# Attention and a rational MLP on one core: the last 64 keys' exponentials are added to the sum tiles by GpSimd instead of being summed by TensorE

## The chip, the core and the metric

The kernel runs on one core of a Trainium2 chip. The metric is device time in microseconds for one execution, median of three runs. TensorE (PE) multiplies matrices, VectorE (DVE) and ScalarE (ACT) work on tiles, GpSimd (POOL) and SyncE (SP) mostly issue DMAs here. Every engine runs its instructions in the order in which they were written, and waits for the others by semaphores. TensorE's weight loads (PEld) are shown beside its products.

## What is computed

Four batches of twelve heads, 448 tokens, head dimension 64. The twelve heads' outputs are put side by side and go through an MLP with a rational activation.

```python
scores = cap * np.tanh(scale * np.matmul(q, k.transpose(0, 1, 3, 2)) / cap)
attn = np.exp(scores - np.max(scores, axis=-1, keepdims=True))
attn = attn / (np.sum(attn, axis=-1, keepdims=True) + 1e-09)
x = np.matmul(attn, v)                 # (4, 12, 448, 64) -> (1792, 768)
h = x @ w_in                           # 768 -> 2048
P = a[0] + a[1] * h + a[2] * h**2 + a[3] * h**3
Q = 1.0 + abs(b[0]) * abs(h) + abs(b[1]) * h**2
out = (P / (Q + 1e-06)) @ w_out        # 2048 -> 768
```

## The kernel before

**Units.** `attention` goes over 24 head pairs p (two heads each). The 448 keys of a head pair are four tiles: n = 0, 1, 2 of 128 keys each, and the last 64 keys, n = 3, for which an even and the next odd head pair share one tile of 128 partitions (64 each). Two head pairs so form a pair k = p // 2, twelve in all. For each tile: `scores` (six products, twelve for n = 3) writes a bank of `ps`, `softmax` has ACT take tanh and then exp into `etiles` (L440, L457). Since the cap bounds the scores, no maximum is subtracted.

**The sums.** For each head pair DVE adds the exponentials of n = 0, 1, 2 into a sum tile `es` (two adds, L463; six such tiles, in `arena_f` and `extra`). The denominators are products of these tiles with a matrix of ones: `norm4` (L594) takes two pairs at once in three rounds of four products into `mi` (plain fp32: each shows as two records in the trace, eight a round). Rounds one and two read the sum tiles, round three reads the shared tiles of the last 64 keys. It stands at p = 5, 9, 13, 17 and 21, behind the scores of n = 3. `norm` (L556) does one pair in two rounds of four, the second over the last 64 keys; it stands at p = 23 for pair 10, and behind the attention for pair 11.

**Behind the sums.** DVE copies `mi` to SBUF (L598), POOL sends it by four small DMAs into a layout of 56 columns, DVE takes the reciprocal (L606), POOL stores it to DRAM (`dn`) and reads it back as broadcasts (`arena_r<-dn`), and DVE multiplies the attention output by them (`xout`, L627). Between these POOL also loads the V rows of the last 64 keys (`ring<-in_v`, `load32`), which wait for the products that read the ring before (L528).

**Other work of a head pair.** `prep_k` and `prep_q` transpose the keys and queries of a later head pair into a bank of `ps` (L343 to L366), from which DVE makes four tiles (L350, L381, L351, L384); the bank is wanted again by that visit's or the next one's third group of scores. `pv` (L511) and `pv_tails` (L528) multiply by V into `pv` and `mi`, which DVE copies out (L535). `split_x` makes an upper part (ACT, L638) and a lower part (DVE, L639) of each 128-column slice of x, and weights are made from 64-bit words early on (L789 to L822).

**The MLP.** `stage1` multiplies a slice of x (upper, lower, upper) with a weight's parts into `ps`, 896 tokens wide, as 512 and 384 columns. For units 0 to 3 it goes slice by slice with the widths in turn (L858); from unit 4 on all 18 products of one width stand in a row (L843). `rational` (L889 to L902) makes the activation, `stage2` (L928) multiplies by w_out. Units 0 and 1 need the first half of the tokens, units 2 and 3 the second, whose last two slices wait for pair 11's denominators.

**What sets the order.** `visits` lists, for each head pair, the functions in order; all TensorE work carries a key `turn`, so TensorE keeps this order. `Plan.flush` then simulates the five engines with the costs given to `op` (`SC_NS`, `PV_NS`, `D_NS`, ...), and writes each engine's instructions in the order in which they start there: the costs decide how ACT's, DVE's, POOL's and SP's rows interleave.

Of the kernel before, what the change touches and what calls it, by code (L numbers as in the profile page):

```python
# [16 lines left out]
ALU = mybir.AluOpType  # L17
# [30 lines left out]
FILL = (4, 4)  # L48
# [24 lines left out]
class Plan:  # L73
# [174 lines left out]
class Body:  # L248
# [11 lines left out]
    def __init__(self, tc, io, cst, bounded):  # L260
# [71 lines left out]
    def prep_k(self, p):  # L332
# [16 lines left out]
        self.op(PE, 440 + SHAPE_NS, tk, self.raw_keys(p, "rk"), [bk, "turn"], early=E_TR)  # L349
# [4 lines left out]
    def prep_q(self, p):  # L354
# [19 lines left out]
        self.op(PE, 390, tq, self.raw_keys(p, "rq"), [bq, "turn"], early=E_TR)  # L374
# [40 lines left out]
    def scores(self, p, n):  # L415
# [15 lines left out]
        first = n == 0 or p % 2 and n == 2  # L431
        self.op(PE, SC_NS * len(sets) + TURN_NS * first, run, [k for name, _ in sets for k in K(name)], w, early=E_SC)

    def softmax(self, p, n):
# [6 lines left out]
        if self.bounded:  # L441
            self.exp(p, n, e, [ek], e, ek)

    def etile(self, p, n):
# [4 lines left out]
        return self.e[ie], ("e", ie)  # L449

# [46 lines left out]
    def pv(self, p):  # L497
# [16 lines left out]

        self.op(PE, PV_NS + SHAPE_NS, run, [("rv", ring_of(g), 0)] + [t[1] for t in tiles], [pk, "turn"])

    def pv_tails(self, p):
# [14 lines left out]
        self.op(PE, TAIL_NS, run, [("v32", ring_of(g), 0), ("v32", ring_of(g), 1), ek], ["pv", "mi", "turn"])  # L532
# [5 lines left out]
    def norm(self, k):  # L538
# [10 lines left out]

        def sums():  # L550
            for last in range(2):
                for j in range(2):
                    for x in range(2):
                        h = 32 * (2 * j + x)
                        st, mv = (self.half[x], tail[:, j]) if last else (self.ones, es[x][:, j])
                        m = nc.tensor.matmul(D[h:h + 32], st, mv, start=not last, stop=last == 1)  # L556
            return m

        self.op(PE, D_NS + SHAPE_NS, sums, [("es", (2 * k + x) % NES) for x in range(2)] + [tk, "ones"], [dk, "turn"])
# [20 lines left out]
    def norm4(self, k):  # L580
# [4 lines left out]
        tails = [self.etile(2 * (k + y), 3) for y in range(2)]  # L585
# [748 lines left out]
```

## Time and profile before

| | us |
|---|---|
| median of 3 runs (lowest to highest) | 660.5 (659.9 to 661.07) |
| the profiled execution | 659.91 |
| its span, first to last instruction | 657.9 |

| engine | busy us | share of the span |
|---|---|---|
| PE | 647.8 | 98% |
| PEld | 542.0 | 82% |
| DVE | 541.9 | 82% |
| ACT | 442.2 | 67% |
| POOL | 85.0 | 13% |

The granted TensorE clock is 0.999 of full speed. Busy times are unions of the instructions' spans; PE's ends are modelled, so the start of the next instruction is the surer end of one. Attention takes the span up to some 184 us, the passage (units 0 to 3 of the MLP) up to some 220, the rest is the MLP.

### The profile page before, as it was taken

How to read it: one execution, taken by the hardware profiler on the slowest of the kernel's cores; microseconds unless marked ns; L12 is line 12 of the kernel's file. 1: busy time of each engine (PE TensorE's matmuls, PEld its weight loads, DVE VectorE, ACT ScalarE, POOL GpSimd, SP SyncE). 2: the span in 40 equal slices, each digit the busy share in tenths (PEclk: the TensorE clock that was granted, in tenths of full speed). 3: DMA queues.
4: the chain of work that ended last, by engine and by line, in shares of the span. 5: the costliest groups of instructions: out<-in, count | busy, mean ns of one | idle time of the engine just before them, and what ended most of it. 6: DMA issues, size and time to landing. Idle time of an engine off the chain costs nothing.

```text
span 657.9 us, 9767 instructions
## 1 busy us (share of the span) xinstructions
PE 647.8 (98%) x3820; PEld 542.0 (82%) x3820; DVE 541.9 (82%) x662; ACT 442.2 (67%) x531; POOL 85.0 (13%) x141
## 2 busy tenths in 40 slices
PE   8999999999999999999999999999999999999996
PEld 5555555655478899999999999999999999999996
DVE  4789899899679987977987897899699789969653
ACT  5899999999857867875457466646646565663560
POOL 4013222321200000020012002101200210120030
PEclk9999999999999999999999999999999999999999
DMA  7757864943230332195158118614821671481086
GB/s 170 186 138 171 203 163 100 199 119 85 59 86 22 128 141 92 51 197 113 48 106 158 49 49 152 158 43 86 166 68 49 128 142 60 95 170 33 1 139 203
DMA packets 79095, 74.45 MB, mean 113 GB/s; under 512 B 48456, under 2 KB 67264, under 8 KB 79040
## 3 DMA queue, kind: packets, MB, share of 16 engines
q1 hardware_dynamic: 68240, 48.68, 25.7%
q0 software_dynamic: 9648, 24.80, 22.5%
q8 instruction: 32, 0.52, 0.3%
q10 hardware_dynamic: 1152, 0.25, 0.2%
q14 instruction: 23, 0.19, 0.1%
HBM read 47.98 MB, written 25.65 MB: 112 GB/s over the span
## 4 chain that ended last, share of the span: by engine, by line
PE 82%; DVE 6%; ACT 4%; DMA 3%; issue 3%; POOL 0%; SPq 0%; DVEq 0%; POOLq 0%; ACTq 0%
PE ps L843 31%; PE ps L928 17%; PE mi L928 9%; PE pv L928 9%; PE ps L429 6%; PE mi L511 3%; DMA arena_r<-dn 2%; ACT etiles L440 2%; PE mi L594 1%; PE pv L511 1%; ACT etiles L457 1%; PE pv L528 1%; PE ps L343 1%; DMA dn<-arena_f 1%; PE ps L366 1%
## 5 line engine op out<-in xcount | busy, mean ns | idle before, releaser
L843 PE MATMUL ps<-arena_r,ring 128*128 128x512 f32 (+1 forms) x924 | 207.6, 363 | 0.0
L843 PEld LDWEIGHTS ps<-arena_r,ring 128*128 128x128 f32 x924 | 167.7, 188 | 17.5
L295 POOL DMA_DIRECT2D out_dram<-arena_f x49 | 42.0, 863 | 423.6 <-ACT arena_f L955 423.6
L928 PE MATMUL ps<-arena_r,etiles 128*128 128x384 f32 x462 | 89.7, 335 | 0.6 <-ACT arena_f L955 0.5
L457 ACT ACTIVATE etiles<-etiles,acap 128x896 f32<-128x896 f32 x84 | 85.5, 1053 | 0.2
L440 ACT ACTIVATE etiles<-ps 128x896 f32<-128x896 f32 x84 | 74.7, 921 | 13.9 <-PE ps L429 13.7
L928 PEld LDWEIGHTS ps<-arena_r,etiles 128*128 128x128 f32 x462 | 80.8, 188 | 1.3 <-ACT arena_f L955 0.8
L928 PE MATMUL mi<-arena_r,etiles 128*128 128x384 f32 x231 | 77.2, 336 | 0.0
L928 PE MATMUL pv<-arena_r,etiles 128*128 128x384 f32 x231 | 77.0, 335 | 0.0
L429 PEld LDWEIGHTS ps<-arena_r 64*128 64x128 f32 x576 | 51.0, 184 | 25.2 <-ACT etiles L457 7.8
L889 ACT ACTIVATE arena_f<-ps,b 128x896 f32<-128x896 f32 x32 | 32.3, 1009 | 54.8 <-PE ps L843 54.7
L429 PE MATMUL ps<-arena_r 64*128 64x448 f32 x576 | 67.7, 376 | 1.2 <-DVE arena_r L384 0.9
L789 ACT ACTIVATE arena_f<-arena_f 128x768 f32<-128x768 f32 x32 | 29.4, 918 | 44.1 <-DMA arena_f<-in_moe_w_out_dram 31.0
L901 ACT CAST etiles<-arena_f 128x896 fp32r<-128x896 f32 x32 | 30.3, 946 | 42.0 <-DVE arena_f L900 42.0
L893 DVE SCALAR_TENSOR_TENSOR arena_f<-arena_f,bab 128x896 f32<-128x896 f32 x32 | 36.8, 1150 | 23.8 <-ACT arena_f L890 23.8
L898 DVE SCALAR_TENSOR_TENSOR arena_f<-arena_f,one 128x896 f32<-128x896 f32 x32 | 36.7, 1148 | 11.3 <-ACT arena_f L896 11.3
L928 PEld LDWEIGHTS pv<-arena_r,etiles 128*128 128x128 f32 x231 | 43.3, 188 | 0.6
L928 PEld LDWEIGHTS mi<-arena_r,etiles 128*128 128x128 f32 x231 | 43.3, 188 | 0.6
L928 PE MATMUL ps<-ring,etiles 128*128 128x384 f32 x210 | 42.0, 334 | 0.0
L902 DVE TENSOR_TENSOR etiles<-arena_f,etiles 128x896 fp32r<-128x896 f32 x32 | 34.9, 1089 | 7.0 <-ACT etiles L901 6.8
L891 ACT ACTIVATE arena_f<-ps,a 128x896 f32<-128x896 f32 x32 | 35.3, 1104 | 3.5 <-DVE arena_f L899 3.5
L897 DVE SCALAR_TENSOR_TENSOR arena_f<-arena_f,a,ps 128x896 f32<-128x896 f32 x32 | 36.6, 1144 | 0.4
(145 smaller groups left out, 1124.2 us busy)
## 6 DMA issues: line engine op xcount, KB each, us to landing
out_dram<-arena_f POOLq DMA_DIRECT2D x49, 384.0 KB, 6.2
arena_f<-in_moe_w_out_dram SPq DMA_DIRECT2D x16, 768.0 KB, 4.3
arena_f<-in_moe_w_in_dram SPq DMA_DIRECT2D x16, 768.0 KB, 4.8
out_dram<-arena_f SPq DMA_DIRECT2D x13, 384.0 KB, 2.5
ring<-in_q_dram SPq DMA_DIRECT2D x44, 112.0 KB, 3.6
arena_r<-dn POOLq DMA_DIRECT2D x20, 224.0 KB, 5.3
ring<-in_k_dram SPq DMA_DIRECT2D x33, 128.0 KB, 3.1
ring<-in_v_dram SPq DMA_DIRECT2D x11, 384.0 KB, 3.7
```

The lines of the kernel that those rows point to most:

```text
L295: self.op(eng, (625 if local else 450) if eng == SP else 1050, lambda: e.dma_start(out, in_, **accum), r, w, nbytes=nbytes, **kw)
L429: m = nc.tensor.matmul(self.PS[i][:, j, 0:448], st[r], mv[r], start=y == 0, stop=y == len(ops) - 1)
L440: self.op(ACT, act_ns(896, True), lambda: nc.scalar.activation(e, ps, AF.Tanh), pk + ["table"], [ek], early=E_TANH)
L457: self.op(ACT, act_ns(size, sk[0][0] == "ps", 1), lambda: nc.scalar.activation(e, src, AF.Exp, scale=acap), sk + ["table"], [ek])
L843: r = nc.tensor.matmul(po[:, ts], w[:, y, kc], mv, start=kc == 0 and z == 0, stop=kc == KC - 1 and z == 2)
L889: self.op(ACT, act_ns(n, True, 1), lambda: T.activation(Bt, h, AF.Abs, scale=b[:, 0:1]), hk, bk)
L891: self.op(ACT, act_ns(n, True, 2), lambda: T.activation(A, h, AF.Identity, scale=a[:, 3:4], bias=a[:, 2:3]), hk, ak)
L893: self.op(DVE, dve_ns(n, 1), lambda: stt(Bt, C, bab[:, 1:2], Bt, ALU.mult, ALU.add), ck + ["bab"], bk)
L897: self.op(DVE, dve_ns(n, 1), lambda: stt(A, A, a[:, 1:2], h, ALU.add, ALU.mult), hk, ak)
L898: self.op(DVE, dve_ns(n, 1), lambda: stt(Bt, Bt, one, C, ALU.add, ALU.mult), ck, bk)
L902: self.op(DVE, dve_ns(n), lambda: V.tensor_tensor(GL(), A, f32(GH()), ALU.subtract), ak + K("gh", ig), K("gl", ig))
L928: r = nc.tensor.matmul(po[n][:, 0:384], st, mv[:, 384 * n:384 * n + 384], start=(y == 0 and x == 0), stop=(y == self.NCH - 1 and x == 2))
```

## The change

Four things, all in the branch for a bounded cap.

- `add_tails`: once ACT has written the last 64 keys' exponentials of a pair and DVE the two sum tiles, GpSimd adds the 64 partitions of each head pair to that head pair's sum tile: two adds of 64 x 896 for each pair but the last, 22 in all. `norm4` loses its third round (five times), `norm` for pair 10 its second. Pair 11 keeps both.
- The order of visits is written as a table of words, `ORDER`; `FILL` goes into it.
- The planner's costs are new; a price for the change from one kind of product to another is asked from `turn`, by what stood before.
- `stage1` for units 0 to 3 takes the three products of a slice for 512 columns and then the three for 384.

```diff
+ORDER = {
+    "odd": "s0 s1 s2 score3 sums4 tanh3 k:2 q:2 pv:-1",
+    -1: "s0 s1 pv:-1 sums s2 t",
...
-SC_NS = 615
-TURN_NS = 200
-SHAPE_NS = 130
-PV_NS = 2220
-TAIL_NS = 870
-D_NS = 1430
-D4_NS = 2210
+SC_NS = 621
+SHAPE_NS = 165
+PV_NS = 2240
+TAIL_NS = 746
+D_NS = 1493
+D4_NS = 2240
...
-        self.free = [4500.0, 4600.0, 3700.0, 3700.0, 9900.0]
-        self.dma_free = 11000.0
+        self.free = [4500.0, 4600.0, 3700.0, 3700.0, 8800.0]
+        self.dma_free = 10000.0
...
+        if self.bounded and n > 1 and p % 2:
+            self.add_tails(p, "s2" if n == 2 else "t")
...
+    def add_tails(self, p, part):
+
+        nc = self.nc
+        self.parts.add((p, part))
+        if p == self.B * self.NP - 1 or not {(p, "s2"), (p, "t")} <= self.parts:
+            return
+        e, ek = self.etile(p, 3)
+        for x in range(2):
+            r, t = p - 1 + x, slice(64 * x, 64 * x + 64)
+            o, a = self.es[r % NES][t], e[t]
+            self.op(POOL, 2100, lambda o=o, a=a: nc.gpsimd.tensor_tensor(o, o, a, ALU.add), [ek], [("es", r % NES)])
...
+        whole = self.bounded and not end
...
-            for last in range(2):
+            for last in range(1 if whole else 2):
...
-            for last in range(3):
+            for last in range(2):
                 for y in range(2):
                     for j in range(2):
                         h = 32 * (2 * y + j)
-                        st, mv = (self.both, tails[y][0]) if last == 2 else (self.unit[last], self.es[es[2 * y + last][1]])
-                        m = nc.tensor.matmul(D[h:h + 32], st, mv[:, j], start=not last, stop=last == 2)
+                        m = nc.tensor.matmul(D[h:h + 32], self.unit[last], self.es[es[2 * y + last][1]][:, j],
+                                             start=not last, stop=last == 1)
...
-                for z, (y, mv) in enumerate(((0, h), (0, lo), (1, h))):
-                    for ts, x in zip(parts, mv):
-                        r = nc.tensor.matmul(po[:, ts], w[:, y, kc], x,
+                for ts, *x in zip(parts, h, lo, h):
+                    for z, y in enumerate((0, 0, 1)):
+                        r = nc.tensor.matmul(po[:, ts], w[:, y, kc], x[z],
```

PE at p = 13, before: the last two groups of scores into `ps`, the sums into `mi`, then the transposes of a later head pair.

```order
L429 MATMUL ps_127<-arena_r 128x448 x6
L429 MATMUL ps_128<-arena_r 128x448 x12
L594 MATMUL mi<-arena_f 32x448 x2
L594 MATMUL mi<-extra,arena_f 32x448 x2
L594 MATMUL mi<-arena_f 32x448 x2
L594 MATMUL mi<-extra,arena_f 32x448 x2
L594 MATMUL mi<-etiles,arena_f 32x448 x4
L343 MATMUL ps_129<-ident,ring_142 128x128 x3
```

The same place after:

```order
L442 MATMUL ps_127<-arena_r 128x448 x6
L442 MATMUL ps_128<-arena_r 128x448 x12
L621 MATMUL mi<-arena_f 32x448 x2
L621 MATMUL mi<-extra,arena_f 32x448 x2
L621 MATMUL mi<-arena_f 32x448 x2
L621 MATMUL mi<-extra,arena_f 32x448 x2
L355 MATMUL ps_129<-ident,ring_142 128x128 x3
```

The round over `etiles` is gone, and nothing else on PE has moved in the attention.

POOL from p = 13 to p = 17, before: the sums' small DMAs (`arena_f<-arena_f`), loads of V tails (`ring`), the store of the reciprocals (`dn`) and the broadcasts (`arena_r<-dn`).

```order
L295 DMA arena_f<-arena_f 16x1x56 x4
L295 DMA ring_141<-in_v_dram 64x2x64
L295 DMA dn<-arena_f 64x56
L295 DMA ring_141<-in_v_dram 64x2x64
L295 DMA arena_r<-dn 64x896 x4
L295 DMA ring_142<-in_v_dram 64x2x64 x2
```

After:

```order
L307 DMA arena_f<-arena_f 16x1x56 x4
L475 TENSOR_TENSOR arena_f<-arena_f,etiles 64x896 x2
L307 DMA ring_141<-in_v_dram 64x2x64
L307 DMA dn<-arena_f 64x56
L307 DMA ring_141<-in_v_dram 64x2x64
L307 DMA arena_r<-dn 64x896 x4
L475 TENSOR_TENSOR arena_f<-arena_f,etiles 64x896 x2
L307 DMA ring_142<-in_v_dram 64x2x64 x2
```

The adds of pairs 6 and 7 stand behind the small DMAs and behind the broadcasts; a V load and the store come behind the first two.

DVE in the passage, before: the activation of units 0 and 1 (L893 to L898), two multiplications by pair 11's reciprocals (L627), the last two splits of the second half (L639).

```order
L893 SCALAR_TENSOR_TENSOR arena_f<-arena_f,bab 128x896
L895 TENSOR_TENSOR arena_f<-ps_127,arena_f 128x896
L791 TENSOR_SCALAR arena_f<-arena_f 128x768
L897 SCALAR_TENSOR_TENSOR arena_f<-arena_f,a,ps_127 128x896
L627 TENSOR_TENSOR arena_f<-arena_r,arena_f 128x448 x2
L898 SCALAR_TENSOR_TENSOR arena_f<-arena_f,one 128x896
L639 TENSOR_TENSOR arena_r<-arena_f,extra 128x896
L639 TENSOR_TENSOR arena_r<-arena_f,arena_r 128x896
```

After:

```order
L921 SCALAR_TENSOR_TENSOR arena_f<-arena_f,bab 128x896
L923 TENSOR_TENSOR arena_f<-ps_127,arena_f 128x896
L925 SCALAR_TENSOR_TENSOR arena_f<-arena_f,a,ps_127 128x896
L926 SCALAR_TENSOR_TENSOR arena_f<-arena_f,one 128x896
L927 SCALAR_TENSOR_TENSOR arena_f<-arena_f,a 128x896
L819 TENSOR_SCALAR arena_f<-arena_f 128x768
L655 TENSOR_TENSOR arena_f<-arena_r,arena_f 128x448 x2
L928 SCALAR_TENSOR_TENSOR arena_f<-arena_f 128x896
L921 SCALAR_TENSOR_TENSOR arena_f<-arena_f,bab 128x896
L667 TENSOR_TENSOR arena_r<-arena_f,extra 128x896
L667 TENSOR_TENSOR arena_r<-arena_f,arena_r 128x896
```

The two splits come behind three more instructions of the activation (L927, L928 and unit 1's L921).

## Rows read from the trace of the kernel before

**Rows 1.** The page's chain that ended last, shares by engine

```profile
PE 82%; DVE 6%; ACT 4%; DMA 3%; issue 3%; POOL 0%; SPq 0%; DVEq 0%; POOLq 0%; ACTq 0%
```

**Rows 2.** Stretches: length, busy PE, PEld, DVE, ACT, POOL, clock, DMA share, GB/s

```profile
69.60:85.00 15.40, 15.15 (x120) 8.25 (x118) 15.40 (x23) 14.04 (x17) 3.48 (x6) 1.00 0.68 177
85.00:99.47 14.47, 14.40 (x108) 8.04 (x106) 13.83 (x23) 13.46 (x16) 4.05 (x7) 1.00 0.71 182
...
127.57:143.54 15.97, 15.72 (x122) 8.22 (x120) 15.96 (x24) 15.50 (x19) 3.48 (x6) 1.00 0.61 132
...
219.73:652.30 432.57, 432.57 (x2328) 411.43 (x2328) 353.71 (x392) 254.15 (x318) 41.97 (x49) 1.00 0.46 104
```

**Rows 3.** The chain in order of time around 127 us: start, us, what

```profile
126.72 0.06 DVE arena_f L627
```

**Rows 4.** DVE in order of time: start, us, instruction, idle before and releaser

```profile
88.00 0.55 DVE L791 TENSOR_SCALAR arena_f<-arena_f 128x768 int32<-128x768 int32 x1
...
123.38 1.09 DVE L463 TENSOR_TENSOR arena_f<-arena_f,etiles 128x896 f32<-128x896 f32 x1
126.72 0.62 DVE L627 TENSOR_TENSOR arena_f<-arena_r,arena_f 128x448 f32<-128x448 f32 x1 [2.25 <-DMA arena_r<-dn]
...
129.05 0.68 DVE L384 SCALAR_TENSOR_TENSOR arena_r<-ps,c,arena_r 128x448 fp32r<-128x448 f32 x1
```

**Rows 5.** PE in order of time, scores of p = 17 and of p = 18

```profile
128.48 3.40 PE L429 MATMUL ps<-arena_r 64*128 64x448 f32 x30
...
139.36 0.87 PE L429 MATMUL ps<-arena_r 64*128 64x448 f32 x6 [0.25 <-DVE arena_r L384]
```

**Rows 6.** The chain in order of time in the passage

```profile
175.90 1.64 PE mi L556 x16
...
186.61 5.14 DMA arena_r<-dn
...
202.30 2.00 DVE arena_r L639 x2
```

**Rows 7.** PE in order of time in the passage

```profile
203.73 0.57 PE L858 MATMUL ps<-extra,ring 128*128 128x512 f32 x2
...
204.97 0.57 PE L858 MATMUL ps<-arena_r,ring 128*128 128x512 f32 x2
...
219.73 2.38 PE L928 MATMUL ps<-arena_r,etiles 128*128 128x384 f32 x12 [0.53 <-ACT arena_f L955]
```

**Rows 8.** PE in order of time, the sums of p = 17 and of p = 23

```profile
133.37 0.94 PE L594 MATMUL mi<-etiles,arena_f 128*32 128x448 f32 x8
134.24 0.55 PE L343 MATMUL ps<-ident,ring 128*128 128x128 f32 x3
...
176.60 0.94 PE L556 MATMUL mi<-etiles,arena_f 128*32 128x448 f32 x8
177.47 0.87 PE L429 MATMUL ps<-arena_r 64*128 64x448 f32 x6
```

**Rows 9.** POOL in order of time

```profile
1.27 0.29 POOL masks.py:199 TENSOR_SCALAR_AFFINE_SELECT ident<-ident 128x128 f32<-128x128 f32 x1
...
42.08 0.59 POOL L295 DMA_DIRECT2D ring<-in_v_dram  x1 [32.62 <-PE mi L528]
...
58.24 0.55 POOL L295 DMA_DIRECT2D dn<-arena_f  x1
...
87.89 0.77 POOL L295 DMA_DIRECT2D dn<-arena_f  x1
```

**Rows 10.** ACT in order of time, the last two exponentials of p = 15

```profile
121.34 1.99 ACT L457 ACTIVATE etiles<-etiles,acap 128x896 f32<-128x896 f32 x2
```

**Rows 11.** The chain in order of time, products of one width in stage 1

```profile
222.11 4.12 PE ps L843 x18
...
230.41 3.12 PE ps L843 x18
```

**Rows 12.** Waits: engine and line, waited for, us in total, times, longest

```profile
DVE arena_f L627 <- DMA arena_r<-dn: 8.5, 3, 3.5
```

More of the change, by code (lines that the diff above doesn't have):

```diff
@@ L47 @@
 WARM2 = (2, 1, 3)
-FILL = (4, 4)
+ORDER = {
[5 rows of a table added]
+}
 Q_ACT = ()
@@ L430, in run @@
             return m
-        first = n == 0 or p % 2 and n == 2
-        self.op(PE, SC_NS * len(sets) + TURN_NS * first, run, [k for name, _ in sets for k in K(name)], w, early=E_SC)
+        self.op(PE, SC_NS * len(sets) + self.turn("s"), run, [k for name, _ in sets for k in K(name)], w, early=E_SC)
     def softmax(self, p, n):
@@ L513, in run @@
             return m
-        self.op(PE, PV_NS + SHAPE_NS, run, [("rv", ring_of(g), 0)] + [t[1] for t in tiles], [pk, "turn"])
+        self.op(PE, PV_NS + self.turn("pv"), run, [("rv", ring_of(g), 0)] + [t[1] for t in tiles], [pk, "turn"])
     def pv_tails(self, p):
@@ L530, in run @@
             return m
-        self.op(PE, TAIL_NS, run, [("v32", ring_of(g), 0), ("v32", ring_of(g), 1), ek], ["pv", "mi", "turn"])
+        self.op(PE, TAIL_NS + self.turn("tails"), run, [("v32", ring_of(g), 0), ("v32", ring_of(g), 1), ek], ["pv", "mi", "turn"])
         for x in range(2):
@@ L555, in sums @@
                         st, mv = (self.half[x], tail[:, j]) if last else (self.ones, es[x][:, j])
-                        m = nc.tensor.matmul(D[h:h + 32], st, mv, start=not last, stop=last == 1)
+                        m = nc.tensor.matmul(D[h:h + 32], st, mv, start=not last, stop=last == 1 or whole)
             return m
-        self.op(PE, D_NS + SHAPE_NS, sums, [("es", (2 * k + x) % NES) for x in range(2)] + [tk, "ones"], [dk, "turn"])
+        self.op(PE, (D_NS // 2 if whole else D_NS) + self.turn("sums"), sums,
+                [("es", (2 * k + x) % NES) for x in range(2)] + [tk] * (not whole) + ["ones"], [dk, "turn"])
         self.op(DVE, dve_ns(448), lambda: nc.vector.tensor_copy(DB, D), [dk], ["db"], early=E_EV)
@@ L592, in sums @@
                         h = 32 * (2 * y + j)
[L593 to L594 removed]
+                        m = nc.tensor.matmul(D[h:h + 32], self.unit[last], self.es[es[2 * y + last][1]][:, j],
+                                             start=not last, stop=last == 1)
             return m
[L597 removed]
+        self.op(PE, D_NS + self.turn("sums"), sums, [*es, "ones"], [dk, "turn"])
         self.op(DVE, dve_ns(448), lambda: nc.vector.tensor_copy(DB, D), [dk], ["db"], early=E_EV)
@@ L685, in visits @@
                         (tails, p), (norm, p // 2)]
-            if p == 0:
-                return [s0, s1, (k, 1), (q, 1), s2, (self.fill, FILL[0])]
-            if p == 1:
-                return [s0, (self.fill, FILL[1]), s1, (k, 2), s2, t, (q, 2), (k, 3), (q, 3), (pv, 0)]
-            if not p % 2:
-                return [s0, s1, s2, *new, (pv, p - 1), (tails, p - 1)]
-            sums = (norm, p // 2 - 1)
-            if p == P1 - 1:
-                return [s0, s1, (pv, p - 1), sums, s2, t]
-            four = [(norm4, p // 2 - 2)] * (p % 4 == 1)
-            return [s0, s1, s2, (self.scores, p, 3), *four, (self.softmax, p, 3), *new, (pv, p - 1)]
+            text = ORDER.get(p if p in ORDER else p - P1) or ORDER["odd" if p % 2 else "even"]
+            out = []
+            for w in text.split():
+                name, _, d = w.partition(":")
+                d = int(d or 0)
+                if name in ("k", "q") and p + d >= P1 or name == "sums4" and p % 4 != 1:
+                    continue
+                out.append(dict(s0=s0, s1=s1, s2=s2, t=t, k=(k, p + d), q=(q, p + d), pv=(pv, p + d), tails=(tails, p + d),
+                                sums=(norm, p // 2 - 1), score3=(self.scores, p, 3), tanh3=(self.softmax, p, 3),
+                                sums4=(norm4, p // 2 - 2), fill=(self.fill, d))[name])
+            return out
         for p in range(P1):
```

14 lines of the change are left out of this document (9 added, 5 removed), and 3 rows, old and new, of the table ORDER.

## The prediction

> **What bounds the kernel now.** I read the chain of work that ended last first, then the busy time by stretch, then the order of time on TensorE (PE) and VectorE (DVE) where the diff edits something. PE carries 82% of the chain [rows 1]. From 219.73 to 652.30 us PE is busy for the whole of the stretch [rows 2]; the diff leaves that part's order as it was, so 432.6 of the 657.9 us are fixed and only the attention and the passage into the MLP can move. In the attention PE is nearly full as well, but DVE is close behind it: 15.40 of 15.40 us in one stretch, 15.96 of 15.97 in another [rows 2]. At 126.72 the chain leaves PE: the multiplication by the broadcast reciprocals starts there after DVE has stood for 2.25 us, and from it DVE work runs without a break until PE, itself late by 0.25 us, goes on at 139.36 [rows 3 to 5]. The chain leaves PE once more: from the sums at 175.90 over the broadcast DMA at 186.61 and a row of DVE and ACT work to PE at 219.73, which had been standing for 0.53 us [rows 6, 7]. Between those two points PE's own work is not what sets the end.
>
> **The removed products.** The third round of the five big sums takes 134.24 - 133.37 = 0.87 us, the second round of the one small sum that changes 177.47 - 176.60 = 0.87 [rows 8]. Of this some belongs to the change to the next kind of product, which stays; I take 0.8, with 0.87 as the upper end. Six times that is 4.8. Five of the six lie where the chain runs on PE. The sixth, at 133.37, lies beside the DVE work of 126.72 to 139.36, so it frees nothing: 5 x 0.8 = 4.0 us gained (3.5 to 5.2).
>
> **DVE's room.** Where DVE is full it can't follow a faster PE. The stretches 69.60:85.00 and 85.00:99.47 hold 15.40 + 13.83 = 29.23 us of DVE work in 29.87 [rows 2]; less 0.8 of PE that is 29.07. I give 0.2 back (0 to 0.8). The stretch at 127.57 was counted as no gain already.
>
> **The added work on GpSimd.** For 11 of the 12 pairs of head pairs two adds of 64 partitions x 896 elements: 22 instructions. No row shows one. From below: the same add on DVE, 1.09 us [rows 4]. From above: GpSimd's one elementwise instruction with an SBUF input, 0.29 us for 128 elements [rows 9], times 7 is 2.03. It is GpSimd's own, so I take 2.0; 22 x 2.0 = 44 us on an engine that is busy for 3.5 us of a 15 us stretch [rows 2]. The adds of pair 7 can start when ACT ends its last exponential, 121.34 + 1.99 = 123.33 [rows 10]; the sums that read them come behind 30 score products that end at 128.48 + 3.40 = 131.88 [rows 5]. So 8.5 us lie there for 4.0 of adds, and for the wait of the second add for DVE's own last add into that tile (to 124.47 [rows 4]). PE doesn't wait for them. The tiles that they hold are written again two pairs (tails) and three pairs (sum tiles) later: no wait. In POOL's queue they stand behind the sums' small DMAs and ahead of the V tails' loads, the reciprocals' store and the broadcasts. Those wait for PE and DVE anyway, and POOL has the time. The first adds come while POOL stands idle until 42.08 [rows 9]; whatever it takes to make the engine ready for this kind of instruction is hidden there. Cost of the queue: 0.
>
> **What the adds do to DVE.** This is the term that no row of this trace prices. The adds run while DVE works on SBUF. The nearest row is POOL's store of the reciprocals: 0.77 us at 87.89, beside a DVE instruction that reads and writes SBUF at 88.00, and 0.55 at 58.24 [rows 4, 9]. That is a hold of 0.22 us, and of POOL, not DVE. Lower end 0; upper end a DVE instruction that stands for the whole of an add, 2.0. I take 0.22, the only hold that a row shows, at three places without slack on DVE, 126.72 and 139.36 [rows 4, 5] and the one other wait for a broadcast in the attention [rows 12]: 0.7 us lost.
>
> **The passage into the MLP.** The new costs move DVE's and ACT's rows (the third pair of fences). From 219.73 back, the chain is as long as before: counted from DVE's first instruction of unit 0 to the last of unit 1 the same instructions stand there. But the last two splits of the second token half (202.30 to 204.30 before [rows 6]) now come behind three more instructions of unit 0 and 1, of about 1.0 us each like the splits, so the lower part of the fifth slice is ready at about 203.3 + 3.0 = 206.3. PE wanted it at 204.97 [rows 7] and now wants it some 0.6 us earlier: as the second product of its slice instead of the third pair, and behind 16 shorter slices. PE waits about 1.9 us there. Of this 0.53 is the stand before 219.73 [rows 7] that it eats up, and 0.5 is the runs of three; the evictions behind it are spread too. I take 0.5 lost (0 to 1.3).
>
> **Runs of three.** Six products of a slice take 204.97 - 203.73 = 1.24 us in alternation [rows 7]. Products of one width in a row take 4.12/18 = 0.229 and 3.12/18 = 0.173 [rows 11], so 3 of each are 1.207, plus two changes of width instead of six. A change costs (1.240 - 1.207)/6 = 0.0055; saved are 4 x 0.0055 = 0.022 a slice, 0.5 us for 24 slices. These slices lie between 179 and 214 us, where the chain isn't on PE: 0 (up to 0.5). The table of orders gives the sequence that the code gave before: 0.
>
> **Sum.** -4.0 + 0.2 + 0.7 + 0.5 = -2.6 us. The profiled execution took 659.91 us, 2.0 around its span of 657.9; less 2.6 that is 657.3. It lies 0.6 below the median of the three runs, 660.5, so on the median: 657.9.
>
> **Rivals.** *The adds hold DVE for their whole length (slower).* The place is pair 7: the first add meets DVE's add at 123.38, the second starts behind that at about 126.5 and the multiplication that is released at 126.72 would stand until 128.4, 1.7 us. Behind it stand the four preparations, the last of which reads its bank until 129.05 + 0.68 = 129.73; PE's third group of scores wants that bank at 128.48 + 12/30 of 3.40 = 129.84 [rows 4, 5]. With 0.1 of slack nearly all of it reaches PE. Such a wait for the broadcast stands twice in the attention (three times in all, 8.5 us [rows 12], one of them behind it): 3.4 us. The other nine pairs lose between 0 and 1.8 each; with 0.5 that is 4.5. In place of my 0.7 the holds cost 7.9: 660.5 - 3.3 + 7.9 = 665.1. It turns slower than before once the holds exceed 3.3 us in all. For it: DVE's adds and multiplications with two SBUF inputs fill much of each pair. Against it: DVE stands for 2.25 us just there, most adds have a slack of some microseconds behind them, and the row at 87.89 shows a short hold, on the other engine.
>
> The Trainium skill, "SBUF — State Buffer", section "Who interferes with whom", says that a VectorE instruction with two SBUF inputs and a GpSimd instruction that reads SBUF exclude each other: whichever starts second stands until the other is done. By that rule this rival's time is the one to expect unless the adds fall into gaps. The row at 87.89 agrees that the engines meet at all; no row here shows VectorE held.
>
> *The gain turns into waits for DVE or ACT (same).* Half-length holds, or more places like 126.72 where DVE or ACT is next late, take 2 to 4.6 us in place of 0.7: between 659.2 and 661.8. For it speak the full DVE stretches of [rows 2].
>
> *The sums wait for the adds (slower).* If an add takes over 4 us, two don't fit into 8.5 us, and PE stands at each of five sums for 1 us or more: 660.5 + 3 or above. Against it: it would be twice my upper row.
>
> *More is gained.* All six rounds at 0.87 and no loss: 655.3.
>
> **How the numbers follow.** Forecast 0.46 (own range 656 to 659.2), more gained 0.04, same 0.20, holds 0.25, waiting sums 0.05. Measurements of this kernel can tell 0.2%, 1.3 us, from no change. So faster 0.50, same 0.20, slower 0.30. The range leaves out the very best and the worse half of the two slow cases: 655.5 to 664.5.
>
> **What would show it.** Right: the sums take about 1.6 us, no PE wait behind GpSimd, pairs with sums 0.8 us shorter, DVE adds still 1.08 us. Wrong: DVE instructions of twice their length, or standing, beside GpSimd's adds, and PE waits for DVE at the third group of scores; or a PE wait for GpSimd at the sums; or a PE gap at about 202 us of more than 2 us.

## The result, and the profile after

The changed kernel takes 667.48 us (median of 6 runs, 665.77 to 668.15), the kernel before 659.92 us beside it (658.85 to 661.07): a ratio of 1.011, 95% interval 1.0097 to 1.0122. It is 7.6 us slower. The prediction said 657.9 us, and its range ended at 664.5: the sign was wrong, and the time lies outside the range. The rival that let GpSimd's adds hold DVE had 665.1.

The profiled execution took 665.77 us, its span is 663.9. From the page: busy time by engine, then the chain of work that ended last.

```profile
PE 647.2 (97%) x3772; PEld 541.3 (82%) x3772; DVE 557.8 (84%) x662; ACT 442.1 (67%) x531; POOL 146.2 (22%) x163
...
PE 74%; DVE 15%; DMA 4%; ACT 3%; issue 3%; SPq 0%; DVEq 0%; ACTq 0%
```

Against [rows 1] PE's share of the chain fell from 82 to 74% and DVE's rose from 6 to 15%. DVE executes the same instructions as before but is busy for 557.8 us instead of 541.9: 15.9 us more for the same work. The groups of DVE instructions between 10 and 190 us show which ones grew. Columns: line, engine, operation, output<-input, shapes, count | busy us, mean ns | idle time before. Two groups of the kernel before, then the changed kernel:

```profile
L463 DVE TENSOR_TENSOR arena_f<-arena_f,etiles 128x896 f32<-128x896 f32 x16 | 17.4, 1084 | 1.1 <-ACT etiles L457 0.8
L463 DVE TENSOR_TENSOR arena_f<-etiles 128x896 f32<-128x896 f32 x16 | 17.3, 1084 | 0.8 <-ACT etiles L457 0.8
```

```profile
L489 DVE TENSOR_TENSOR arena_f<-arena_f,etiles 128x896 f32<-128x896 f32 x16 | 22.6, 1411 | 1.3 <-ACT etiles L483 0.8
L489 DVE TENSOR_TENSOR arena_f<-etiles 128x896 f32<-128x896 f32 x16 | 20.2, 1265 | 0.0
L393 DVE TENSOR_SCALAR arena_r<-ps,c 128x448 fp32r<-128x448 f32 x21 | 14.0, 668 | 0.0
L655 DVE TENSOR_TENSOR arena_f<-arena_r,arena_f 128x448 f32<-128x448 f32 x18 | 12.1, 691 | 0.0
L633 DVE TENSOR_SCALAR arena_f<-arena_f,guard 64x56 f32<-64x56 f32 x5 | 7.8, 1554 | 0.0
```

In the kernel before, L655 (there L627) has a mean of 614 ns, and L633 (there L605) 235. The preparation L393, whose input is in PSUM (`ps`), hasn't changed: 668 against 674. What grew is DVE's work from SBUF to SBUF: additions and multiplications with both inputs there, and tensor-scalars such as the guard's small addition.

One place shows how. (An engine stands while it waits; a hold is the time by which an instruction is longer than the shortest of its form.) First DVE, then GpSimd (POOL), then PE in order of time (start, us, instruction, in brackets the idle time before and who ended it); the last three lines are stretches: length, busy PE, PEld, DVE, ACT, POOL, granted clock, DMA share, GB/s.

```profile
21.47 0.68 DVE L393 TENSOR_SCALAR arena_r<-ps,c 128x448 fp32r<-128x448 f32 x1
22.06 2.92 DVE L489 TENSOR_TENSOR arena_f<-etiles 128x896 f32<-128x896 f32 x1
24.91 0.67 DVE L396 SCALAR_TENSOR_TENSOR arena_r<-ps,c,arena_r 128x448 fp32r<-128x448 f32 x1
...
21.93 2.10 POOL L475 TENSOR_TENSOR arena_f<-arena_f,etiles 64x896 f32<-64x896 f32 x1 [14.22 <-ACT etiles L483]
...
25.63 1.08 PE L442 MATMUL ps<-arena_r 64*128 64x448 f32 x6 [2.24 <-DVE arena_r L396]
28.43 3.02 PE L537 MATMUL mi<-etiles,arena_f 128*64 128x448 f32 x12
...
24.00:26.00 2.00, 0.37 (x4) 0.35 (x6) 2.00 (x3) 1.48 (x2) 0.60 (x2) 1.00 0.66 171
26.00:28.00 2.00, 2.00 (x13) 1.49 (x10) 0.58 (x1) 1.25 (x2) 1.33 (x1) 0.54 1.25 256
28.00:30.00 2.00, 2.00 (x9) 0.83 (x9) 1.39 (x3) 1.53 (x2) 1.31 (x2) 0.61 0.13 20
```

GpSimd's add runs from 21.93 to 24.03. DVE's add, issued at 22.06, ends at 24.98, which is 0.95 after GpSimd has finished: it stood still until then. Behind it in DVE's queue is the second half of the queries' preparation (L396); PE wants that and stands for 2.24 us (0.40 before). After this stand the granted clock falls to the lower of its two levels (1.2 in place of 2.4 GHz; the stretches show 0.54 and 0.61 as means), and twelve products that take 2.48 us elsewhere take 3.02. By 32.3 us the kernel is 3.7 us behind, 0.3 of which it had from its start: 3.4 us from one add.

The other way round the same happens: 22 adds of 2.1 us are 46.2 us, but GpSimd's adds are busy for 61.6 (16 x 2.616 + 6 x 3.282), so GpSimd too stood for some 15 us.

Not all that DVE does from SBUF to SBUF is held. A reciprocal beside a GpSimd add wasn't, though it too goes from SBUF to SBUF, with one input: it keeps its 0.49 us, which it has before as well (GpSimd, then DVE).

```profile
177.58 2.11 POOL L475 TENSOR_TENSOR arena_f<-arena_f,etiles 64x896 f32<-64x896 f32 x1 [1.10 <-DVE arena_f L633]
...
177.63 0.49 DVE L634 RECIPROCAL arena_f<-arena_f 64x56 f32<-64x56 f32 x1
```

How far each kernel is ahead of or behind the kernel before, at the start of the last key transpose of head pair n and at the stand of PE that ends the passage [rows 7] (us; minus is earlier; the last three kernels are experiments below):

| place (time before) | after | one column | first pair | third rounds back |
|---|---|---|---|---|
| n = 3 (18.59) | +0.3 | +0.1 | +0.8 | +0.1 |
| n = 5 (32.27) | +3.7 | +0.1 | +0.8 | +0.1 |
| n = 11 (77.49) | +4.3 | -1.3 | +1.4 | -0.4 |
| n = 16 (111.43) | +5.5 | -1.8 | +2.6 | +0.1 |
| n = 19 (134.62) | +5.7 | -2.7 | +2.8 | +0.7 |
| n = 23 (163.67) | +6.5 | -3.8 | +3.6 | +1.2 |
| MLP (219.73) | +5.4 | -4.9 | +4.1 | +0.1 |

### The profile page after: what moved, and what is told of

Its sections match the earlier page's. It is cut to its first block, busy times and chain, and to the rows that moved or that the text cites. A ratio compares the mean times of both kernels' runs of the same rounds, so it can differ in the third digit from the quotient of the medians.

```text
span 663.9 us, 9749 instructions
## 1 busy us (share of the span) xinstructions
PE 647.2 (97%) x3772; PEld 541.3 (82%) x3772; DVE 557.8 (84%) x662; ACT 442.1 (67%) x531; POOL 146.2 (22%) x163
## 4 chain that ended last, share of the span: by engine, by line
PE 74%; DVE 15%; DMA 4%; ACT 3%; issue 3%; SPq 0%; DVEq 0%; ACTq 0%
PE ps L871 29%; PE ps L956 16%; PE mi L956 8%; PE pv L956 8%; PE ps L442 4%; DVE arena_f L489 3%; PE mi L537 2%; DMA arena_f<-in_moe_w_out_dram 2%; DVE arena_r L396 1%; DVE arena_r L362 1%; DVE arena_r L393 1%; DMA arena_r<-dn 1%; PE pv L537 1%; DVE arena_f L655 1%; DVE extra L489 1%
## 5 line engine op out<-in xcount | busy, mean ns | idle before, releaser
L442 PE MATMUL ps<-arena_r 64*128 64x448 f32 x576 | 69.7, 379 | 5.7 <-DVE arena_r L396 5.5
L917 ACT ACTIVATE arena_f<-ps,b 128x896 f32<-128x896 f32 x32 | 32.3, 1009 | 55.8 <-PE ps L871 53.6
L921 DVE SCALAR_TENSOR_TENSOR arena_f<-arena_f,bab 128x896 f32<-128x896 f32 x32 | 36.7, 1147 | 23.1 <-ACT arena_f L918 23.1
L475 POOL TENSOR_TENSOR arena_f<-arena_f,etiles 64x896 f32<-64x896 f32 x16 | 41.9, 2616 | 36.6 <-ACT etiles L483 26.8
L926 DVE SCALAR_TENSOR_TENSOR arena_f<-arena_f,one 128x896 f32<-128x896 f32 x32 | 36.7, 1147 | 11.3 <-ACT arena_f L924 11.3
```

What stands on the lines that cost most here:

```text
L442: m = nc.tensor.matmul(self.PS[i][:, j, 0:448], st[r], mv[r], start=y == 0, stop=y == len(ops) - 1)
L475: self.op(POOL, 2100, lambda o=o, a=a: nc.gpsimd.tensor_tensor(o, o, a, ALU.add), [ek], [("es", r % NES)])
L917: self.op(ACT, act_ns(n, True, 1), lambda: T.activation(Bt, h, AF.Abs, scale=b[:, 0:1]), hk, bk)
L921: self.op(DVE, dve_ns(n, 1), lambda: stt(Bt, C, bab[:, 1:2], Bt, ALU.mult, ALU.add), ck + ["bab"], bk)
L926: self.op(DVE, dve_ns(n, 1), lambda: stt(Bt, Bt, one, C, ALU.add, ALU.mult), ck, bk)
```

## The experiments

Theory "hold": a DVE instruction that needs SBUF for both inputs (or is a tensor-scalar from SBUF to SBUF, as the guard's addition) and a GpSimd instruction that reads SBUF exclude each other. Rivals: "order" (the new costs and the table moved DVE and ACT rows and that costs), and "queue" (GpSimd's occupied time delays the small stores and broadcasts behind it). Code is shortened, and line numbers shift by a few from kernel to kernel: DVE's add is L489, L491 or L494.

**One column.** Against the changed kernel:

```
-nc.gpsimd.tensor_tensor(o, o, a, ALU.add)
+nc.gpsimd.tensor_tensor(o[:, :, 0:1], o[:, :, 0:1], a[:, :, 0:1], ALU.add)
```

> The GpSimd adds stay where they are, with all that they wait for and all that waits for them, but each adds 1 column of 448 instead of all (the other 447 columns of the last 64 keys are left out of these sums). The order on every engine is that of the changed kernel. Theory 'hold' (a DVE instruction that takes both inputs from SBUF, or goes from SBUF to SBUF as a tensor-scalar, stands until the GpSimd add beside it has ended): DVE's adds are back at 1.08 us, the tensor-scalar of the guard at 0.24, the PE stand of 2.24 us at 25.63 is gone with the fall of the clock behind it, and the time is about 656 us (removed products 4.0 below 659.9, passage 0 to +0.5). Theory 'order' (the new costs and the table moved DVE and ACT rows, and that is what is lost): the time stays at 665 to 668 us. Theory 'queue' (the adds' place in GpSimd's queue, ahead of the small stores and broadcasts) would also give 656, and the next kernel tells it from 'hold'.

Measured: 655.86 us, 0.9951 of before (0.9924 to 0.9977). The same groups of DVE as above:

```profile
L489 DVE TENSOR_TENSOR arena_f<-arena_f,etiles 128x896 f32<-128x896 f32 x16 | 17.4, 1085 | 1.3 <-ACT etiles L483 0.8
L489 DVE TENSOR_TENSOR arena_f<-etiles 128x896 f32<-128x896 f32 x16 | 17.3, 1079 | 0.4 <-ACT etiles L483 0.4
L655 DVE TENSOR_TENSOR arena_f<-arena_r,arena_f 128x448 f32<-128x448 f32 x22 | 12.9, 614 | 5.6 <-DMA arena_r<-dn 5.6
L633 DVE TENSOR_SCALAR arena_f<-arena_f,guard 64x56 f32<-64x56 f32 x5 | 1.2, 234 | 0.0
```

All are back to their length. With every instruction in its place and every wait kept, the length of the adds is worth (667.48 - 659.92) + (660.08 - 655.86) = 11.8 us by the medians, and 10.5 by the two ratios. "Order" falls.

**Fills, which read nothing.**

```
-nc.gpsimd.tensor_tensor(o, o, a, ALU.add)
+nc.gpsimd.memset(o, 1.0); nc.gpsimd.memset(o, 1.0)
```

> In place of each GpSimd add stand two GpSimd fills with 1.0 of the same 64 x 896 tile, which write SBUF and read nothing (the sums' upper or lower 64 rows are overwritten, so the sums are other numbers). Waits and order are those of the changed kernel; I expect about 1 us for one fill, 2 us for both, as long as an add. Theory 'hold' (it is GpSimd's reading that stops DVE): no DVE instruction is lengthened, about 656 to 657 us. Theory 'queue' (GpSimd's time is what costs, since its DMAs stand behind): 665 us or more, with DVE rows at their old length and DVE waits for broadcasts. If writing alone holds DVE as well: DVE adds beside fills lengthened as in the changed kernel, 665 us or more.

Measured: 656.38 us, 0.9942 (0.9926 to 0.9959). A fill and the DVE adds beside it, in order of time:

```profile
81.15 0.84 POOL L474 MEMSET arena_f<- 64x896 f32 x1
82.05 0.84 POOL L475 MEMSET arena_f<- 64x896 f32 x1
...
81.36 1.08 DVE L494 TENSOR_TENSOR arena_f<-etiles 128x896 f32<-128x896 f32 x1
82.36 0.62 DVE L660 TENSOR_TENSOR arena_f<-arena_r,arena_f 128x448 f32<-128x448 f32 x1
```

GpSimd is occupied for 1.7 us in each add's place and writes twice as much; DVE keeps its 1.08 and 0.62. So neither the queue nor the writing costs: "queue" falls too, and what is left is GpSimd's reading. There is one exception, too small to show in the time: beside a tensor-scalar from SBUF to SBUF (L824) a fill took 1.14 instead of 0.84 us, at two places, and that instruction at one of them 0.74 instead of 0.55.

```profile
38.76 1.14 POOL L475 MEMSET arena_f<- 64x896 f32 x1
...
38.38 0.74 DVE L824 TENSOR_SCALAR arena_f<-arena_f 128x768 int32<-128x768 int32 x1 [0.58 <-DMA ring<-in_q_dram]
```

**One input.**

```
-nc.gpsimd.tensor_tensor(o, o, a, ALU.add)
+nc.gpsimd.tensor_copy(o, a)
```

> In place of each add stands a GpSimd copy of the last 64 keys' exponentials into the same half of the sum tile (one SBUF input instead of two; the sum of the other keys is lost in these rows). Waits and order are those of the changed kernel. If any GpSimd instruction that reads SBUF holds DVE for its length: a copy of 1 to 2 us, DVE adds and the guard's tensor-scalar lengthened by up to that, 660 to 666 us in proportion. If only two inputs do, as DVE's own instructions with one input from PSUM aren't held: about 656 us, as with the fills.

Measured: 656.45 us, 0.996 (0.9947 to 0.9973). By its time alone this would speak for "only two inputs hold". The rows say otherwise (GpSimd, then DVE):

```profile
21.90 0.93 POOL L475 COPY arena_f<-etiles 64x896 f32<-64x896 f32 x1 [14.19 <-ACT etiles L483]
...
22.05 1.72 DVE L489 TENSOR_TENSOR arena_f<-etiles 128x896 f32<-128x896 f32 x1
```

The copy ends at 22.83, DVE's add 0.94 later: held as before, but for 0.8 us. DVE is busy for 546.0 us, 4.9 more than with one column, and the time rises by only 0.6 (by the ratios) to 1.5 us (by the medians against their own runs of before). Holds of under a microsecond were mostly swallowed by DVE's slack. The expectation tied the mechanism to the time (660 to 666 us if a reading copy holds), and only the rows could separate them.

**Third rounds back.** The five big sums and the small one get their last round back, and the adds go; table, costs and runs of three stay.

```
-if self.bounded and n > 1 and p % 2:
-    self.add_tails(p, "s2" if n == 2 else "t")
...
-        whole = self.bounded and not end
+        whole = False
...
-            for last in range(2):
+            for last in range(3):
...
```

> The third rounds of products are back in all sums and there are no GpSimd adds; the table of orders, the new costs and the runs of three stay. Theory 'hold': 659.5 us, the time before less up to 0.5 for the runs of three. Theory 'order' (costs and table lose the time): 665 us or more.

Measured: 660.57 us, 1.0004 (0.9988 to 1.002): no difference that can be told. The rest of the change is neutral for the whole time. In the trace that is made of two parts: 1.2 us lost by n = 23, 1.1 gained in the passage.

**The first pair alone.** Its two adds go, and its two products come back.

```
-if p == self.B * self.NP - 1 or not {(p, "s2"), (p, "t")} <= self.parts:
+if p in (1, self.B * self.NP - 1) or not {(p, "s2"), (p, "t")} <= self.parts:
...
```

> The first pair of head pairs goes back to the third round of products (2 products, some 0.4 us of PE); its two GpSimd adds at 21.9 and 26.7 us go; the other ten pairs keep theirs. Order on DVE and ACT is that of the changed kernel. Theory 'hold': the DVE add at 22.06 takes 1.08 instead of 2.92 us, the second half of the queries is prepared 1.8 us earlier, PE's stand at 25.63 shrinks from 2.24 to 0.4 us, the granted clock doesn't fall at 26 to 29 us, and 3.4 us that were lost by 32.3 us are back: less 0.4, about 664.5 us. If the loss at one place is merely handed on (DVE being the bound later anyway, so that an earlier start is spent in waits): 666 to 667.5 us.

Measured: 663.53 us, 1.0066 (1.0032 to 1.0101); the interval is wide, since two of nine executions took 669.8. PE, and a stretch behind it:

```profile
24.24 0.88 PE L442 MATMUL ps<-arena_r 64*128 64x448 f32 x6 [0.40 <-DVE arena_r L396]
...
26.00:28.00 2.00, 2.00 (x13) 0.77 (x12) 1.80 (x4) 2.00 (x3) 0.00 (x0) 1.00 1.09 234
```

The clock stays up. Behind n = 7 this kernel is 2.9 us ahead of the changed one, at n = 9, 13, 18 and 23 alike: what was lost at one place in the first pair was handed on through the attention, undiminished. In the passage 1.6 of the 2.9 go again (+5.4 and +4.1 at the MLP); the times of the whole kernels differ by 2.9 us by the ratios. So the rival "merely handed on into waits" falls for the attention; how much reaches the end is known only within the interval.

**Two halves.** Each add in two pieces of 448 columns.

```
-self.op(POOL, 2100, lambda o=o, a=a: nc.gpsimd.tensor_tensor(o, o, a, ALU.add), [ek], [("es", r % NES)])
+for j in range(2):
+    o, a = self.es[r % NES][t, j], e[t, j]
+    self.op(POOL, 1050, lambda o=o, a=a: nc.gpsimd.tensor_tensor(o, o, a, ALU.add), [ek], [("es", r % NES)])
```

> Each GpSimd add of 64 x 896 becomes two of 64 x 448, one for each head of the pair of heads; the work and the result are the same. Theory 'hold, instruction by instruction' (whichever of the two engines starts second stands until the other's instruction has ended): a piece takes about 1.05 us by itself, no DVE instruction stands longer than that, and pieces fit better between DVE's instructions that read PSUM. DVE's excess over before (15.9 us in the changed kernel) falls to some 10 us and the time to about 664 us. If the two engines share the path access by access, cutting changes nothing: 667 to 668 us with DVE's excess as it was.

Measured: 663.28 us, 1.0063 (1.0047 to 1.008). The guard's addition, and the same first place as above:

```profile
L635 DVE TENSOR_SCALAR arena_f<-arena_f,guard 64x56 f32<-64x56 f32 x5 | 5.0, 1005 | 0.0
...
21.69 1.95 DVE L491 TENSOR_TENSOR arena_f<-etiles 128x896 f32<-128x896 f32 x1
...
24.29 0.87 PE L442 MATMUL ps<-arena_r 64*128 64x448 f32 x6 [1.27 <-DVE arena_r L396]
```

A held instruction now stands for one piece: 1.95 in place of 2.92, 1005 ns in place of 1554 (the longest hold is 1.22 us). DVE is busy for 554.9 us, only 2.9 less than with whole adds, because it is held more often, 19 times instead of 11; yet 3.4 us come back (4.1 above the kernel before instead of 7.6). No PE stand was followed by a fall of the clock here (1.27, 1.37 and 1.68 us were the longest).

**Twice.** Each add issued twice in a row (the last 64 keys count twice).

```
-nc.gpsimd.tensor_tensor(o, o, a, ALU.add)
+nc.gpsimd.tensor_tensor(o, o, a, ALU.add); nc.gpsimd.tensor_tensor(o, o, a, ALU.add)
```

> Each GpSimd add is issued twice in a row, so the last 64 keys count twice in these sums. From one column to all columns the time rose from 655.9 to 667.5 us, 11.6 for 46 us of adds. Theory 'hold': as much again, about 678 us, and more if the sums then wait for GpSimd (four adds of 2.1 us and their own holds no longer fit into the 8.5 us ahead of the sums): up to 685. If DVE's and PE's slack is used up only by some first part and the rest is hidden, or if the holds are a fixed cost for each meeting: 668 to 672 us.

Measured: 700.34 us, 1.0627 (1.0609 to 1.0644), 33 us for the second 46 us of adds, where the first 46 cost 11.8. The expectation of 678 to 685 missed: the slack was used up, and PE's stands grew (2.2 to 2.9 us at six places). The sums did wait for GpSimd, as the expectation said, but only twice (0.82 and 0.67 us). One of the longest stands, and the clock behind it:

```profile
112.00 1.49 PE L442 MATMUL ps<-arena_r 64*128 64x448 f32 x6 [2.81 <-DVE arena_r L396]
...
112.00:114.00 2.00, 2.00 (x9) 1.41 (x10) 2.00 (x1) 0.47 (x1) 1.92 (x2) 0.50 1.00 229
```

The clock fell four times in the attention. But behind stands of 2.33 us (at 85.12) and 2.23 (at 89.44) it stayed at 1.00.

**The guard in the copy.** Of the changed kernel's eleven holds (17.9 us in all) four fell on the small addition L633, 1.65 us each (the expectation says five). One of them, GpSimd first:

```profile
115.92 6.41 POOL L475 TENSOR_TENSOR arena_f<-arena_f,etiles 64x896 f32<-64x896 f32 x2
...
120.48 1.89 DVE L633 TENSOR_SCALAR arena_f<-arena_f,guard 64x56 f32<-64x56 f32 x1
```

Here the addition is folded into the copy out of PSUM:

```
-nc.vector.tensor_copy(DB, D)
+nc.vector.tensor_scalar(DB, D, guard, None, ALU.add)
 ...
-nc.vector.tensor_scalar(sc, sc, guard, None, ALU.add)
 nc.vector.reciprocal(sc, sc)
```

> The changed kernel with all its GpSimd adds; the small addition of the guard to the sums (64 x 56, SBUF to SBUF, 0.24 us by itself, 1.55 beside the adds) is folded into the copy of the sums out of PSUM, which has its input from PSUM. Theory 'hold': five of the eleven holds of over 1.2 us were this instruction (1.65 us each, 8.2 of 17.9 us); it is gone, and the copy isn't held. If these holds reach PE one to one: 667.5 - 7 = 660 us. If most of them lie in time that DVE has to spare, or another instruction next in DVE's queue is held in its place: 664 to 667 us. I expect 664.

Measured: 668.72 us, 1.0139 (1.0109 to 1.0169). The expected 664 was wrong: nothing came back. DVE is busy for 553.2 us, 4.6 less, but the holds fell on other instructions, on worse places. DVE and PE:

```profile
73.89 2.31 DVE L650 TENSOR_TENSOR arena_f<-arena_r,arena_f 128x448 f32<-128x448 f32 x1 [2.36 <-DMA arena_r<-dn]
159.13 2.99 DVE L662 TENSOR_TENSOR arena_r<-arena_f,arena_r 128x896 fp32r<-128x896 f32 x1
...
78.64 1.69 PE L442 MATMUL ps<-arena_r 64*128 64x448 f32 x14 [1.81 <-DVE arena_r L396]
166.09 2.08 PE L442 MATMUL ps<-arena_r 64*128 64x448 f32 x18 [1.25 <-DVE arena_r L396]
```

L650 is the multiplication by the reciprocals, ahead of the four preparations, a place of the kind that the prediction's rival had named. The guard's addition seems to have been a cheap one to hold, since small stores and a broadcast stand behind it; that isn't shown by itself. The planner also moved some forty DVE rows here, so not all of the difference need be the holds' new places.

**Halves and the guard together.** Both edits.

```
+for j in range(2): (two pieces, as above)
+nc.vector.tensor_scalar(DB, D, guard, None, ALU.add)
```

> Both of it: adds in two pieces of 448 columns and the guard in the copy. In pieces alone the time was 663.3 us, with four holds of some 0.95 us on the guard's addition left. If these matter: 660.5 to 662 us. If not: 663 us. Below the kernel before (659.9 us) only if the remaining holds are hidden, which I don't expect.

Measured: 667.58 us, 1.0119 (1.0093 to 1.0145), 7.9 above the kernel before, where the halves alone were 4.1 above, although DVE is busy for 4.8 us less. At 114 us PE stood for 1.98 us, and the clock fell:

```profile
116.04 0.89 PE L442 MATMUL ps<-arena_r 64*128 64x448 f32 x6 [1.98 <-DVE arena_r L396]
...
118.00:120.00 2.00, 2.00 (x7) 0.76 (x8) 2.00 (x3) 1.74 (x2) 1.88 (x2) 0.50 0.06 13
```

Again the sum of the holds didn't tell the time. With whole adds, the guard in the copy, halves, and both, DVE is busy longer than before by 15.9, 11.3, 13.0 and 8.2 us, and the kernel by 7.6, 9.1, 4.1 and 7.9. PE's stands in the attention come closer (8.4, 8.4, 6.7 and 8.1 us), and only with halves alone did the clock not fall.

**An adding DMA.** Removing the reader: a DMA from GpSimd's queue that adds on its way.

```
-self.op(POOL, 2100, lambda o=o, a=a: nc.gpsimd.tensor_tensor(o, o, a, ALU.add), [ek], [("es", r % NES)])
+self.dma(POOL, o, a, [ek], [("es", r % NES)], accum_op=ALU.add)
```

> Each add is done by a DMA that adds the tail's tile to the sum tile on its way (issued from GpSimd's queue in the same place); no engine reads the tiles, and the result is the same up to rounding. Theory 'hold': no DVE instruction is lengthened, and the products stay removed: about 656 to 657.5 us, below the kernel before. Against it, as a rival: 22 transfers of 229 KB beside the loads; the sums come 8.5 us behind the exponentials, so if such a transfer takes over 8 us, PE stands at the five sums, 3 us or more in all, and the time is 660 us or above.

Measured: 661.14 us (658.92 to 666.08), 1.004 (1.0011 to 1.0068). No DVE instruction was held (541.8 us busy), so the expectation was right on the mechanism and wrong on the time. One of the five sums waited for such a transfer (0.76 us at 107 us), a small part of what the expectation's rival named. At another place DVE stood longer for a broadcast of the reciprocals. DVE, here and in the one-column kernel:

```profile
70.14 0.63 DVE L655 TENSOR_TENSOR arena_f<-arena_r,arena_f 128x448 f32<-128x448 f32 x1 [3.67 <-DMA arena_r<-dn]
```

```profile
68.47 0.62 DVE L655 TENSOR_TENSOR arena_f<-arena_r,arena_f 128x448 f32<-128x448 f32 x1 [1.99 <-DMA arena_r<-dn]
```

That the 22 transfers of 224 KB made this broadcast late is likely, not shown: the twenty broadcasts from GpSimd's queue took 4.7 us from issue to landing (median; 4.9 with one column). Loads did take longer, those of the queries 4.6 instead of 3.5 us, those of V 5.3 instead of 3.8.

**The adding DMA with later multiplications.** The planner reckons more time for such a DMA, and the fourth early weight strip is made a step later; then the same with the guard in the copy.

```
-d0 = max(self.free[e] + (850 if e == SP else 1500), self.dma_free)
+d0 = max(self.free[e] + (850 if e == SP else 2300), self.dma_free)
...
-if (p, m) == (at + 1, 0):
+if (p, m) == (at + 1, x == 3):
```

> The version with adding DMAs (no GpSimd reading, 661.1 us) lost its gain where DVE stood 3.67 us for the broadcast at 70.1 us (1.99 with one-column adds), where ACT stood 3.3 us for a store of weights at 82 us, and in the passage. Here the planner reckons 2300 instead of 1500 ns for a DMA from GpSimd's queue to land, so that the multiplications by the reciprocals come later in DVE's order, and the fourth early weight strip is made one step later. If these were the only losses: 656 to 658 us. If the DMA engines' load is the cause and merely shows elsewhere: 659.5 to 662 us.

> As the one before, and the guard is added in the copy out of PSUM, so that the chain from the sums to the broadcast is 0.24 us shorter and DVE has five instructions less. 0 to 1 us below the one before: 656 to 658 us if its losses were only those named, 659 to 662 if the DMA engines' load is the cause.

Measured: 658.18 us, 0.998 (0.9968 to 0.9993), and with the guard 659.13, 0.9989 (0.9976 to 1.0002). The first lies between the two ranges that its expectation gave; the second, in the range for the DMA engines' load, can't be told from the first. DVE's waits for the broadcasts fell from 8.1 us, in four waits, to one of 0.4 (columns: us in all, times, longest):

```profile
DVE arena_f L655 <- DMA arena_r<-dn: 0.4, 1, 0.4
```

So the first version is faster than the kernel before by 0.2%, at the edge of what can be told; of the 4.2 us that the removed products are worth, 1.5 were kept. Where the rest goes is open in part: PE stands for ACT there three times in the attention (0.79, 1.26 and 0.91 us) and once for DVE (0.76), and which of that the transfers cause wasn't tried apart.

## Why the prediction was wrong, step by step

**What bounds the kernel** was read rightly: PE with DVE close behind. That is why DVE's 15.9 us mattered. One reading was late: the chain leaves PE not at 126.72 but behind the sums that end at 105.78, over GpSimd's DMAs, the store at 116.43 and the broadcast at 120.32. What was missed is how little of a hold the slack takes once holds are long: about 5 us of holds in pieces of 0.5 to 0.8 cost some 1 us (the copies), 15.9 us in pieces of up to 2 cost 11.8.

**The removed products** were sized well: 0.8 each, five of them 4.0. With one column the five big sums gained 0.70 to 0.81 each: 3.8 by n = 23. The placement was wrong by one: the sum at 133.37, counted as no gain, did gain (-1.8 to -2.7 between n = 16 and 19 of the table), and the small one at 176.60, counted as a gain, lies in a passage that gets 1.1 us shorter whether it is removed (one column: -3.8 to -4.9) or not (third rounds back: +1.2 to +0.1). Two errors that cancel: that 4.0 came out is in part luck. The sums in the changed kernel, in answer to [rows 8]:

```profile
138.32 1.71 PE L621 MATMUL mi<-arena_f 128*32 128x448 f32 x16
139.97 0.55 PE L355 MATMUL ps<-ident,ring 128*128 128x128 f32 x3
```

**DVE's room** was put at 0.2 us, which fits: with one column the sums at n = 11 and 15 gained 0.70 and 0.75, and between n = 11 and 12 0.2 went back (from -1.3 to -1.1). **The queue** at 0 was right (fills). An add of 2.0 us was right (2.10). **The sums don't wait for the adds** was right: no product waited for GpSimd in the changed kernel (one weight load stood 0.3 us for an add).

**What the adds do to DVE** is the step that failed. It was put at 0.7 us, three times 0.22, and measured 11.8 (10.5 by the ratios). The 0.22 came from the nearest row, but that row ([rows 9], a GpSimd store at 87.89) issues a DMA; it isn't an instruction that reads SBUF as data. It bounded nothing. The other bound, an instruction that stands for the whole add, was in the text and was the right one: 2.92 at 22.06, 1.89 for a form of 0.23. The number of places was also wrong. Three places without slack had been named; from 20 us to the end of the attention PE stood at twelve places in the changed kernel (8.4 us in all) and at four before (1.7).

**The rival** had the mechanism, and 665.1 against 667.5. Its place was only half right. In pair 7, in answer to [rows 4, 5] (GpSimd, DVE, PE):

```profile
128.91 3.34 POOL L475 TENSOR_TENSOR arena_f<-arena_f,etiles 64x896 f32<-64x896 f32 x1 [1.50 <-ACT etiles L483]
133.35 2.36 POOL L475 TENSOR_TENSOR arena_f<-arena_f,etiles 64x896 f32<-64x896 f32 x1 [1.10 <-DVE arena_f L489]
...
129.22 1.07 DVE L489 TENSOR_TENSOR arena_f<-etiles 128x896 f32<-128x896 f32 x1
130.40 2.80 DVE L489 TENSOR_TENSOR arena_f<-arena_f,etiles 128x896 f32<-128x896 f32 x1
133.12 0.61 DVE L655 TENSOR_TENSOR arena_f<-arena_r,arena_f 128x448 f32<-128x448 f32 x1
...
136.17 2.09 PE L442 MATMUL ps<-arena_r 64*128 64x448 f32 x18 [0.22 <-DVE arena_r L396]
```

The first add met DVE's add, as told, and held it by 1.7 us; the multiplication, for which the rival had counted the 1.7, slipped in 0.2 us ahead of the second add and kept its 0.61, and since the broadcast had long landed there, the 1.7 ate what before was DVE's wait. PE stood for 0.22 there, where before its thirty products ran in a row [rows 5]. The rival priced the other pairs at 0.5 each; the first pair alone cost 3.4, because PE's stand there also brought the clock down, which no step of the prediction had. The Trainium skill, "SBUF — State Buffer", section "Who interferes with whom", had given the rule that decided: whichever starts second stands until the other is done, and for a VectorE instruction with two SBUF inputs only GpSimd instructions that read are concerned. Add (2.92 us in place of 1.08), copy (1.72) and fill (1.08) agree with it. The prediction cited it and then weighed it against one row that didn't test it; 0.25 for this rival was too little.

**The passage** was put at 0.5 lost; in the changed kernel it was 1.1 gained (n = 23 to the MLP, +6.5 to +5.4), and as much with one column and with the third rounds back. In the kernel without the first pair's adds it was 0.5 lost, with a stand of 0.42 us for the late split (L669 there), the mechanism that the prediction had named. In answer to [rows 7], PE's stand before the MLP is as long as before, and no gap stands at the late splits:

```profile
225.17 2.35 PE L956 MATMUL ps<-arena_r,etiles 128*128 128x384 f32 x12 [0.54 <-ACT arena_f L983]
```

How much of the 1.1 is runs of three and how much the moved rows wasn't told apart. **Runs of three and the table** together with the new costs: 0 for the whole time, as said, though with the third rounds back it is 1.2 lost and 1.1 gained.

The sum as measured: -4.2 for all but the adds' length, where the steps gave -3.3, and +11.8 for their length, where they gave 0.7.

## What to carry over

Before work goes to an idle GpSimd, look at what it reads and for how long, not at its free time: with VectorE busy on additions and multiplications that take both inputs from SBUF, each GpSimd instruction that reads SBUF was a lock of its own length here. Keep such instructions short (halves gave 3.4 us back, copies of 0.9 us were nearly free). Judge a hold by what stands behind it in the queue and whether TensorE ends up standing: the sum of the holds said little, TensorE's stands and the falls of its clock said more.

## What was not expected of the hardware

A stand of TensorE of 2.24 us in the midst of full work was followed by some 3 us at the lower granted clock (0.54 and 0.61 in the stretches behind it), and one of 1.98 us by a fall as well. Stands of up to 1.68 us in the version with halves weren't, nor two of 2.33 and 2.23 us with the adds twice, so the length of one stand doesn't settle it; what does wasn't tried. So a late instruction on another engine can cost TensorE nearly twice its own length: 1.84 of hold became 3.4 us.

The record's order of starts doesn't always say who is held: in pair 7, above, GpSimd's add started at 128.91, 0.31 ahead of a DVE add that took its normal 1.07 us, while the GpSimd add took 3.34 instead of 2.10. GpSimd's spans are called rough by the page of the profile, and this may be a case of it.

An adding DMA of 224 KB from SBUF to SBUF landed 4.6 to 5.4 us after its issue (median) and lengthened no DVE instruction. Beside these transfers the loads of the queries and of V landed 1.1 and 1.5 us later (medians) than with one column.
